# A first tile's softmax moved to ScalarE, a second tile loaded in halves, and new orders, in a fused attention and channel-mix kernel

## The chip, the cores and the metric

The kernel runs on one core of one Trainium2 chip. The metric is device time in microseconds (us) for one execution. TensorE (PE) multiplies, VectorE (DVE) and ScalarE (ACT) do the elementwise work, SyncE (SP) issues the DMA transfers, GpSimd (POOL) does almost nothing here. PEld in a row is PE's weight load.

## What is computed

Chunked local attention (batch 4, 8 heads, 768 tokens, head size 64; each chunk of 32 queries sees 16 keys to the left, its own 32, 8 to the right and 8 memory keys, 64 in all), whose output is the input of a channel mix with a squared-ReLU feed-forward and a sigmoid gate. Cut to what matters:

```python
scores = scale * np.matmul(q_c, k_full.transpose(0, 1, 3, 2))
scores = scores - np.max(scores, axis=-1, keepdims=True)
a = np.exp(scores)
a = a / (np.sum(a, axis=-1, keepdims=True) + 1e-09)
out[:, :, c_start:c_end] = np.matmul(a, v_full)
...
x_prev = np.concatenate([np.zeros((B, 1, D), dtype=np.float32), x[:, :-1, :]], axis=1)
xk = mu_k * x + (1.0 - mu_k) * x_prev
xr = mu_r * x + (1.0 - mu_r) * x_prev
k = np.maximum(xk @ w_k, 0.0)
v = k * k @ w_v
r = 1.0 / (1.0 + np.exp(-(xr @ w_r)))
return (r * v).astype(np.float32)
```

## The kernel before

The 3072 tokens are cut into 12 units of 256 tokens, each of two tiles of 128 (tile t belongs to unit t // 2). For a tile the stages are: load of queries and keys (`qk`, L561); scores on PE into the PSUM tile `s` (L588, for tile 0 L670); softmax into `e`; transposes of `e` on PE into `pt` (L751); copies of `pt` into `aTz` (L397); the product with the values (`vw`, L745) into `px` (L771); a copy into `xT` (L397). From unit 3 on the transposes are done by a round trip through DRAM instead: DVE transposes blocks of 32 by 32 (`eT`, L900), SP writes `eD` (L907) and reads it back as `aTz` in four loads (L911). From unit 6 on the product with the values (L843) has its result turned the same way (DVE L850, write of `xD` L856, four loads into `xT` L861). Then come the mix of the unit (`xf`, or its parts `xh` and `xl`), and the three matrix products of the channel mix: `ph` (first layer, L1425 for unit 0, L1454 and L1479 later), `pr` (gate, L1359, L1368), and the second layer (`pv` L1568, L1581 for the first two units, and sums `accx`, `accy`, `accz`, L1270, later). The weights arrive in ten loads w0 to w9 (L445, L447), are put together from two 32-bit words by ACT (absolute value, L465) and DVE (mask L470, join L474), and are then split into two fp32r parts.

The softmax of tile 0 works by halves b of its heads (`first_part`, L645): DVE takes the maximum from PSUM (L679, L681), subtracts it (L688, L690), ACT does one exp over 128x256 (L693), DVE sums (L699); after both halves DVE adds 1e-9, takes the reciprocal (L701, L702) and multiplies (L706). Tile 1 does the same steps whole, 128x512 at a time (`part`, L601, L606, L612, L616 to L618, L622).

What sets the order: PE's order is written by hand, `LEAD` for the first two units, a string of `STAGES` for each later one (unit 0's string is the default). In these, h, g, v and p stand for matrix products of the channel mix, s and z for scores of later units, t, a, b, x for transposes and products with the values: in unit 5's string z is the scores of unit 8 and x the `px` of unit 7. SP's first 23 loads are put in the order of `LOADS` (q0a, q0b: halves of tile 0's load; q1, q2, ...: tiles; v: values; w: weights). Everything else is placed by the planner (`Plan`): it simulates the engines with a cost for each operation, works by due times, and writes the instructions of each engine in the order of its simulated starts; each engine then executes its own list in that order, so that an instruction which waits holds up all that follow it on its engine. The letters of `FORCE` add rules: n, j make norm and join of w0 wait in the plan for steps of tile 1; t puts both copies of tile 1's `pt` on ACT. While PE waits for its first `ph`, the kernel fills in matmuls on zeros (`warm`, L1639).

## Time and profile before

| | us |
|---|---|
| median of 3 runs | 377.25 |
| the runs | 374.96, 377.25, 377.32 |
| the profiled execution, its own time | 376.67 |
| its span, first to last instruction | 374.9 |
| PE busy in the span | 367.7 (98%) |
| DVE busy | 322.7 (86%) |
| ACT busy | 206.2 (55%) |
| DMA engines busy (queue of the data) | 47.8% |

The span is divided by what each engine did; a row of the timeline gives the start, the duration, the engine, the line of the kernel, the operation with output and inputs, and in brackets how long the engine had been idle before and what ended that. The profiled execution's own time is 1.77 us longer than its span. The rows that the argument rests on stand in a section further down.

### The profile page before, as it was taken

The page shows a single profiled execution, that of the slowest core. Times are in us where ns is not written, and L with a number is a line of the kernel's source. Part 1 is how long each engine was busy: PE and PEld are TensorE (multiplying, and loading weights), DVE is VectorE, ACT ScalarE, POOL GpSimd, SP SyncE. Part 2 cuts the span into 40 slices and gives each one's busy share as a digit, 9 for nine tenths or more (in the row PEclk, how much of TensorE's full clock was granted, in tenths as well). Part 3 has the DMA queues.
Part 4 walks back from the last instruction along what each step waited for, and adds up shares of the span by engine and source line. Part 5 has one row for each costly group of instructions (what it writes and reads, how often), then busy time and mean ns, then how long its engine had stood idle before and what let it go on. Part 6 is the DMA issues. An engine that isn't in the chain of part 4 may idle for free.

```text
span 374.9 us, 11497 instructions
## 1 busy us (share of the span) xinstructions
PE 367.7 (98%) x5084; PEld 339.6 (91%) x5084; DVE 322.7 (86%) x524; ACT 206.2 (55%) x307; POOL 2.4 (1%) x9
## 2 busy tenths in 40 slices
PE   7999999999999999999999999999999999999996
PEld 5886579988999999999999998999999999999996
DVE  3899999999999499989699997996998988788274
ACT  2797996954774386475068157238338244156260
POOL 2000000000000000000000000000000000000000
PEclk9999999999999999999999999999999999999999
DMA  7999981324701735556692485266343340400101
GB/s 287 403 417 409 389 309 71 113 87 140 274 39 72 262 120 179 215 165 240 246 278 93 153 288 179 64 220 230 127 154 115 112 169 2 143 30 0 58 1 58
DMA packets 24146, 64.78 MB, mean 173 GB/s; under 512 B 2720, under 2 KB 10784, under 8 KB 23712
## 3 DMA queue, kind: packets, MB, share of 16 engines
q1 hardware_dynamic: 24096, 64.04, 47.8%
q8 instruction: 40, 0.66, 0.7%
q14 instruction: 10, 0.08, 0.1%
HBM read 49.88 MB, written 14.16 MB: 171 GB/s over the span
## 4 chain that ended last, share of the span: by engine, by line
PE 82%; DMA 9%; DVE 5%; SPq 1%; issue 1%; ACT 0%; DVEq 0%
PE ph L1479 26%; PE pr L1368 14%; PE accy L1270 10%; PE accx L1270 7%; PE accz L1270 6%; PE pv L1581 4%; DMA raw<-in_w_k_dram 4%; PE s L588 4%; PE ph L1454 3%; PE px L771 3%; PE px L843 2%; PE pv L1568 2%; DMA qk<-in_qk_dram 2%; DMA aTz<-eD 1%; DMA xT<-xD 1%
## 5 line engine op out<-in xcount | busy, mean ns | idle before, releaser
L1479 PE MATMUL ph<-xh,wk 128*128 128x256 f32 x320 | 89.1, 278 | 0.0
L1479 PE MATMUL ph<-xh,wl 128*128 128x256 f32 x320 | 88.0, 275 | 0.0
L1479 PE MATMUL ph<-xl,wk 128*128 128x256 f32 x320 | 88.0, 275 | 0.0
L1498 ACT ACTIVATE kf<-ph 128x512 f32<-128x512 f32 x47 | 27.6, 596 | 88.7 <-PE ph L1479 88.4
L1479 PEld LDWEIGHTS ph<-xh,wk 128*128 128x128 f32 x320 | 61.4, 192 | 0.8
L1479 PEld LDWEIGHTS ph<-xh,wl 128*128 128x128 f32 x320 | 61.5, 192 | 0.0
L1479 PEld LDWEIGHTS ph<-xl,wk 128*128 128x128 f32 x320 | 61.4, 192 | 0.0
L1215 DVE TENSOR_TENSOR al<-kf,ah 128x512 fp32r<-128x512 f32 x50 | 33.6, 679 | 1.8 <-PE accz L1270 1.6
L1368 PE MATMUL pr<-wr,xh 128*128 128x512 f32 x88 | 34.1, 388 | 0.0
L1368 PE MATMUL pr<-wr,xl 128*128 128x512 f32 x88 | 33.4, 379 | 0.0
L1368 PE MATMUL pr<-wl,xh 128*128 128x512 f32 x88 | 33.4, 379 | 0.0
L397 ACT CAST ah<-kf 128x512 fp32r<-128x512 f32 x45 | 27.3, 620 | 9.7 <-DVE kf L1193 7.2
L1505 ACT ACTIVATE kf<-kf 128x512 f32<-128x512 f32 x45 | 28.1, 632 | 1.1
L1377 ACT ACTIVATE sg_sb<-pr 128x512 f32<-128x512 f32 x24 | 14.0, 597 | 20.5 <-PE pr L1368 20.3
L1270 PE MATMUL accx<-wv,ah 128*128 128x256 f32 x80 | 22.1, 276 | 0.0
L1270 PE MATMUL accx<-wv,al 128*128 128x256 f32 x80 | 22.0, 275 | 0.0
L1270 PE MATMUL accx<-wl,ah 128*128 128x256 f32 x80 | 22.0, 275 | 0.0
L588 PEld LDWEIGHTS s<-qk 64*32 64x32 f32 x1472 | 15.2, 105 | 4.0 <-issue 2.9
L1368 PEld LDWEIGHTS pr<-wr,xh 128*128 128x128 f32 x88 | 16.7, 189 | 2.5
L1368 PEld LDWEIGHTS pr<-wr,xl 128*128 128x128 f32 x88 | 16.6, 189 | 2.3
L1368 PEld LDWEIGHTS pr<-wl,xh 128*128 128x128 f32 x88 | 16.7, 189 | 1.9
L588 PE MATMUL s<-qk 64*32 64x64 f32 x1472 | 17.2, 225 | 1.1 <-DMA qk<-in_qk_dram 1.1
(165 smaller groups left out, 956.0 us busy)
## 6 DMA issues: line engine op xcount, KB each, us to landing
qk<-in_qk_dram SPq DMA_DIRECT2D x23, 768.0 KB, 6.1
vw<-in_vw_dram SPq DMA_DIRECT2D x24, 512.0 KB, 5.2
out_dram<-o SPq DMA_DIRECT2D x23, 256.0 KB, 2.4
eD<-eT SPq DMA_DIRECT2D x9, 512.0 KB, 2.7
aTz<-eD SPq DMA_DIRECT2D x36, 128.0 KB, 3.0
raw<-in_w_v_dram SPq DMA_DIRECT2D x4, 1024.0 KB, 10.2
raw<-in_w_k_dram SPq DMA_DIRECT2D x3, 1024.0 KB, 10.6
xD<-aTz SPq DMA_DIRECT2D x6, 512.0 KB, 2.6
```

Source lines behind the costliest of these rows:

```text
L397: e.copy(dst, src)
L588: nc.tensor.matmul(s5[CHUNK * j : CHUNK * (j + 1), h, d - c, r, :], *operands(ts[d], r, j, slice(64 * h, 64 * h + 64)), start=True, stop=True,
L771: nc.tensor.matmul(p3[64 * h : 64 * h + 64, 2 * g : 2 * g + 2, CHUNK * j : CHUNK * j + CHUNK], v[:, g, h, j, :], a[:, h, g, j, :], start=True,
L1215: nc.vector.tensor_sub(low(n), place[n](), T["ah", u, n].bitcast(F32))
L1270: nc.tensor.matmul(o, x, w, start=(n in fresh and c + i == 0), stop=(c == cs[-1] and i == 2), skip_group_check=True)
L1368: nc.tensor.matmul(pairs(p), x[:, place_of(u)[k], c * P : (c + 1) * P], woven(w), start=(k + n == 0), stop=(k == KT - 1 and n == 2),)
L1377: nc.scalar.activation(sg, p, AF.Sigmoid)
L1454: nc.tensor.matmul(pairs(T["ph", u, f][:, i * UTOK : (i + 1) * UTOK]), w[:, fc], x[:, :, k].rearrange("p t n -> p n t"), start=(i + k + n ...
L1479: nc.tensor.matmul(pairs(p[:, i * UTOK : (i + 1) * UTOK]), w[:, fc], x[:, :, place_of(u)[k]].rearrange("p t n -> p n t"), start=(k + n == ...
L1498: e.activation(part(), p, AF.Relu)
L1505: e.activation(q, q, AF.Square)
L1581: nc.tensor.matmul(pairs(p), x[:, tc_], woven(w), start=(f + n == 0), stop=(f == FT - 1 and n == 2),)
```

## The change

Softmax of tile 0. DVE still takes the maximum of each half, and multiplies it by minus the scale (128x4). ACT then reads the scores from PSUM and does the subtraction inside the exp, its bias being the scaled maximum: as that is another value for each head, one exp of 128x64 for each of the 8 heads (4 to a half), whose second output (`accum_out`) is the sum over the 64 keys. Subtractions and sums are gone from DVE. The scores of the second half now go to banks of the tag `tp` (two of them, by head parity), where they went to one tile of tag `s`.

Tile 1. Its load is cut into two halves (q1a, q1b), and scores, maximum, subtraction, exp and sum go by halves, still the old way (DVE subtracts, one exp, DVE sums).

Orders. `LOADS`: w0 before the identity, w3 before w4, q2 before q3, w7 before v2, w9 before v3. `LEAD`: the scores of unit 1 are split, with a quarter of the last `ph` step between; some further pairs change places. `STAGES`: other strings for all units but 1. `FORCE`: the second half of w0's absolute value now waits for tile 0's two copies of `pt`, and tile 1's copies are no longer kept on ACT. The planner's model of instruction fetches has other constants, v1's load another cost, and the planner's last pass keeps the order in which operations open a buffer tag. Four fp32 matmuls on zeros fewer are issued before the first `ph` (10, before 14).

```diff
-FORCE = "njt"
+FORCE = "njc"
 HALF = 2
-LOADS = "q0a q0b q1 id w0 v0 v1 w1a w1b w2 w4 w3 q3 q2 w5 w6 v2 w7 w8 v3 q4 w9 q5"
...
+FUSED, FUSED_US = (0,), 1.2
+LOADS = "q0a q0b q1a q1b w0 id v0 v1 w1a w1b w2 w3 w4 q2 q3 w5 w6 w7 v2 w8 w9 v3 q4 q5"
...
-    0: "z h0 h2 h3 h1 x g0 p1 p7 p6 p2 p5 g1 p3 p4",
...
+    0: "z h2 h0 h1 h3 x g0 p1 p7 p6 p4 p2 p5 g1 p3",
...
-    5: "h1 z h0 h2 x h3 p1 g0 p7 p6 g1 p5 p2 p4 p3",
...
+    5: "z h0 h1 h2 x h3 g0 p1 p7 p6 g1 p2 p5 p4 p3",
...
-FETCH, FETCH_LEAD, FETCH_US, FETCH_AT, FETCH_FROM, FETCH_RATE = 256, 40, 4.9, 123, 2600, (0.0046, 0.0088)
+FETCH, FETCH_LEAD, FETCH_US, FETCH_AT, FETCH_FROM, FETCH_RATE = 256, 32, 4.0, 123, 2600, (0.0046, 0.0088)
...
+                if s.tag in opened and opened[s.tag] is not o:
+                    edge(opened[s.tag], o)
+                opened[s.tag] = o
...
+            def f_sub(b):
+                if fused:
+                    nc.vector.tensor_scalar_mul(mxs(b), mxs(b), -SCALE)
+                    return
...
+                def sub(h, s):
+                    m = mxs(b)[:, h]
+                    nc.vector.tensor_sub(e4(b)[:, h], s, m.unsqueeze(len(m.shape)).to_broadcast(list(s.shape)))
...
+            def f_exp(b):
+                if not fused:
+                    nc.scalar.activation(e4(b), e4(b), AF.Exp, scale=SCALE)
+                    return
...
+                for h in range(2):
+                    for r in range(R):
+                        g = slice(R * b + r, R * b + r + 1)
+                        nc.scalar.activation(
+                            e4(b)[:, h, r], s4(b, h)[:, r], AF.Exp, bias=pt["mx"][:, h, g], scale=SCALE, accum_out=pt["sum"][:, h, g]
+                        )
+
+            def f_sum(b):
...
+                if not fused:
+                    nc.vector.reduce_sum(sm[:, :, R * b : R * (b + 1)], e4(b), axis=AX.X)
+                if b:
+                    nc.vector.tensor_scalar_add(sm, sm, 1e-9)
+                    nc.vector.reciprocal(sm, sm)
...
-            if t == 0:
-                l.append([op(("dma", 1.05), lambda b=b: f_load(0, b), new=[x] * (b == 0), use=[x] * b, due=0.1 * b) for b in range(2)])
-                loads.update(q0a=l[0][0], q0b=l[0][1])
+            if u == 0:
+                l.append([op(("dma", 1.05), lambda b=b, t=t: f_load(t, b), new=[x] * (b == 0), use=[x] * b, due=0.2 * t + 0.1 * b) for b in range(2)])
+                loads.update({f"q{t}a": l[t][0], f"q{t}b": l[t][1]})
```

Where instructions stand, first on DVE at the start of the program. A name carries its unit or tile, and ends with a buffer number: `mx0_0`, `s0_0_1`, `sum0_0` belong to tile 0, `mx0_1`, `s0_1`, `sum0_1` to tile 1, `e0` to both. Before, from the maximum of tile 0's second half to the last multiplication of tile 1:

```order
L681 TENSOR_REDUCE mx0_0_115<-s0_0_2_96 128x2x2
L690 TENSOR_TENSOR e0_136<-s0_0_2_96,mx0_0_115 128x2x128
L699 TENSOR_REDUCE sum0_0_143<-e0_136 128x2x2 x2
L701 TENSOR_SCALAR sum0_0_143<-sum0_0_143 128x8
L702 RECIPROCAL sum0_0_143<-sum0_0_143 128x8
L601 TENSOR_REDUCE mx0_1_189<-s0_1_148 128x8
L606 TENSOR_TENSOR e0_136<-s0_1_148,mx0_1_189 128x2x256
L706 TENSOR_TENSOR e0_136<-e0_136,sum0_0_143 128x2x256
L616 TENSOR_REDUCE sum0_1_204<-e0_136 128x8
L617 TENSOR_SCALAR sum0_1_204<-sum0_1_204 128x8
L618 RECIPROCAL sum0_1_204<-sum0_1_204 128x8
L622 TENSOR_TENSOR e0_136<-e0_136,sum0_1_204 128x2x256
```

And after the change, from the first maximum of tile 1 on (tile 0's maxima and their multiplication by minus the scale stand ahead of it):

```order
L688 TENSOR_REDUCE mx0_1_170<-s0_1_147 128x2x2
L699 TENSOR_TENSOR e0_140<-s0_1_147,mx0_1_170 128x2x128
L688 TENSOR_REDUCE mx0_1_170<-s0_1_147 128x2x2
L725 TENSOR_SCALAR sum0_0_139<-sum0_0_139 128x8
L726 RECIPROCAL sum0_0_139<-sum0_0_139 128x8
L699 TENSOR_TENSOR e0_140<-s0_1_147,mx0_1_170 128x2x128
L723 TENSOR_REDUCE sum0_1_200<-e0_140 128x2x2
L730 TENSOR_TENSOR e0_140<-e0_140,sum0_0_139 128x2x256
L723 TENSOR_REDUCE sum0_1_200<-e0_140 128x2x2
L725 TENSOR_SCALAR sum0_1_200<-sum0_1_200 128x8
L726 RECIPROCAL sum0_1_200<-sum0_1_200 128x8
L730 TENSOR_TENSOR e0_140<-e0_140,sum0_1_200 128x2x256
```

Tile 0's two sums and three subtractions are gone; tile 1's maximum, subtraction and sum each stand twice, over 128x256, and the multiplication of tile 0 (L706 before, the first L730 now) has moved from before tile 1's sum to between its two parts.

The second place is DVE at the end of unit 5, with the last steps of unit 8's softmax (`e8`), its transposes (`eT8`), and the evacuation of unit 5's results (`o5`). Before:

```order
L622 TENSOR_TENSOR e8_2667<-e8_2667,sum8_0_2969 128x1024
L1312 TENSOR_TENSOR o5_1_2916<-accz5_2897,o5_1_2916 128x256
L1032 TENSOR_TENSOR xl6_0_3017<-df6_2669,xh6_0_2914 128x1024
L1335 TENSOR_TENSOR o5_1_2916<-o5_1_2916,sg_sb_78 128x512
L1312 TENSOR_TENSOR o5_0_2867<-accy5_2920,o5_0_2867 128x256
L1340 TENSOR_TENSOR o5_0_2867<-accx5_2853,sg_sb_78 128x256
L1342 TENSOR_TENSOR o5_0_2867<-o5_0_2867,sg_sb_78 128x256
L900 STREAM_TRANSPOSE eT8_3204<-e8_2667 128x1024
L977 TENSOR_TENSOR df7_3208<-xT7_2998 128x16x63
```

And now:

```order
L629 TENSOR_TENSOR e8_2673<-e8_2673,sum8_0_2928 128x1024
L1252 TENSOR_TENSOR al2_5_2932<-kf5_1_2755,ah3_5_2969 128x512
L1069 TENSOR_TENSOR xl6_0_2986<-df6_2704,xh6_0_2904 128x1024
L1377 TENSOR_TENSOR o5_0_2911<-accx5_2887,sg_sb_78 128x256
L1349 TENSOR_TENSOR o5_1_2934<-accy5_2936,o5_1_2934 128x256
L937 STREAM_TRANSPOSE eT8_3014<-e8_2673 128x1024
L1349 TENSOR_TENSOR o5_1_2934<-accz5_2915,o5_1_2934 128x256
L1372 TENSOR_TENSOR o5_1_2934<-o5_1_2934,sg_sb_78 128x512
L1349 TENSOR_TENSOR o5_0_2911<-accy5_2936,o5_0_2911 128x256
L1379 TENSOR_TENSOR o5_0_2911<-o5_0_2911,sg_sb_78 128x256
```

Before, the transposes `eT8` came after the last instruction on `o5`, with six rows between them and `e8`'s multiplication; now four rows stand between, and four instructions on `o5` come behind the transposes.

The third place is SP's queue behind it. Before:

```order
L1315 DMA out_0_dram<-o5_1_2916 128x512
L1315 DMA out_0_dram<-o5_0_2867 128x512
L907 DMA eD8_3206<-eT8_3204 128x1024
L561 DMA qk20_3212<-in_qk_dram 128x1536
L911 DMA aTz_79<-eD8_3206 32x4x256 x4
L561 DMA qk21_3297<-in_qk_dram 128x1536
L745 DMA vw18_3307<-in_vw_dram 128x1024
```

And now:

```order
L898 DMA xT7_2906<-xD7_2874 32x4x256 x4
L944 DMA eD8_3030<-eT8_3014 128x1024
L1352 DMA out_0_dram<-o5_1_2934 128x512
L1352 DMA out_0_dram<-o5_0_2911 128x512
L948 DMA aTz_79<-eD8_3030 32x4x256 x4
L568 DMA qk20_3141<-in_qk_dram 128x1536
L568 DMA qk21_3176<-in_qk_dram 128x1536
```

The write `eD8` now stands ahead of the two stores of unit 5's output, and the load `qk20` (768 KB), which stood between the write and the four reads `aTz`, now stands behind them.

## Rows read from the trace of the kernel before

**Rows 1.** stretch, its length, busy PE, PEld, DVE, ACT, POOL, PEclk, DMA share, GB/s

```profile
...
0.00:16.56 16.56, 13.87 (x229) 10.62 (x229) 9.54 (x25) 6.97 (x12) 2.33 (x8) 1.00 0.90 338
16.56:224.10 207.54, 207.43 (x2987) 187.64 (x2984) 192.53 (x294) 131.96 (x195) 0.11 (x1) 1.00 0.58 209
224.10:226.10 2.00, 0.82 (x34) 0.50 (x37) 0.73 (x3) 1.69 (x4) 0.00 (x0) 1.00 0.46 177
226.10:371.70 145.60, 145.60 (x1870) 140.87 (x1850) 119.47 (x205) 65.59 (x99) 0.00 (x0) 1.00 0.31 105
```

**Rows 2.** PE's waits, longest first (line, releaser: us in total, times, longest)

```profile
...
PE px L843 <- DMA aTz<-eD: 1.2, 2, 0.6
PE s L588 <- DMA qk<-in_qk_dram: 1.1, 1, 1.1
```

**Rows 3.** timeline of the start (start us, us, engine, line, operation, idle before)

```profile
...
1.18 2.93 PE L1639 MATMUL warm<-zero_sb 128*128 128x256 f32 x6 [1.18 <-DVE zero_sb L387]
...
4.98 0.68 PE L670 MATMUL s<-qk 64*32 64x48 f32 x32 [0.25 <-DMA qk<-in_qk_dram]
...
5.59 1.97 PE L1639 MATMUL warm<-zero_sb 128*128 128x256 f32 x6
...
7.77 0.20 DVE L702 RECIPROCAL sum<-sum 128x8 f32<-128x8 f32 x1
```

**Rows 4.** the timeline going on, 8 to 17 us

```profile
...
8.64 0.85 PE L588 MATMUL s<-qk 64*32 64x64 f32 x64 [1.08 <-DMA qk<-in_qk_dram]
...
9.42 2.43 PE L1639 MATMUL warm<-zero_sb 128*128 128x256 f32 x10
...
12.81 0.69 DVE L622 TENSOR_TENSOR e<-e,sum 128x512 f32<-128x512 f32 x1
...
13.55 0.66 PE L751 MATMUL pt<-id_sb,e 128*128 128x128 f32 x4
...
14.25 1.17 ACT L397 COPY aTz<-pt 64x512 f32<-64x512 f32 x2
14.26 1.23 DVE L474 SCALAR_TENSOR_TENSOR w<-w,raw 128x1024 uint32<-128x1024 uint32 x1
...
15.47 1.15 PE L771 MATMUL px<-aTz,vw 128*64 128x64 f32 x32 [0.18 <-ACT aTz L397]
...
16.56 0.71 PE L1425 MATMUL ph<-xf,w 128*128 128x128 f32 x4
```

**Rows 5.** durations by shape, 0 to 20 us (line, operation, count, busy us, mean ns)

```profile
...
L693 ACT ACTIVATE e<-e 128x256 f32<-128x256 f32 x2 | 0.8, 417 | 4.2 <-DVE e L688 3.7 <-DVE e L690 0.5
...
L950 ACT ACTIVATE xf<-px,mu_sb 128x128 f32<-128x128 f32 x2 | 0.7, 368 | 0.0
...
L681 DVE TENSOR_REDUCE mx<-s 128x4 f32<-128x256 f32 x1 | 0.4, 425 | 0.1
```

**Rows 6.** timeline, 28 to 30 us: PE and its weight loads

```profile
...
28.52 1.32 PEld L588 LDWEIGHTS s<-qk 64*32 64x32 f32 x128 [0.33 <-DMA qk<-in_qk_dram]
28.52 1.48 PE L588 MATMUL s<-qk 64*32 64x64 f32 x128
...
29.93 1.13 PE L1425 MATMUL ph<-xf,w 128*128 128x256 f32 x4
```

**Rows 7.** DVE's timeline before the wait at 225 us

```profile
...
213.63 0.42 DVE L1342 TENSOR_TENSOR o<-o,sg_sb 128x256 f32<-128x256 f32 x1
213.96 1.24 DVE L900 STREAM_TRANSPOSE eT<-e 128x1024 f32<-128x1024 f32 x1
```

**Rows 8.** SP's DMA issues, same stretch (start us, us of issuing)

```profile
...
215.60 0.45 SPq L561 DMA_DIRECT2D qk<-in_qk_dram  x1
218.12 2.88 SPq L911 DMA_DIRECT2D aTz<-eD  x4
```

**Rows 9.** chain that ended last, 200 to 230 us (start us, us, what)

```profile
...
220.56 5.28 DMA aTz<-eD
```

**Rows 10.** DMA issues, from the page's last part (count, KB each, median us to landing)

```profile
...
aTz<-eD SPq DMA_DIRECT2D x36, 128.0 KB, 3.0
```

More of the change, by code (lines that the diff above doesn't have):

```diff
@@ L151, in place @@
             if eng == "pe":
-                cost, _ = self.fetched(t, cost, port)
+                o.ready = max([0.0] + [e + HOP[g] for e, g in ready if g != "pe"])
+                cost, _ = self.fetched(t, cost, port, o.ready)
             elif port:
```

154 lines of the change are left out of this document (80 added, 74 removed), and 10 rows, old and new, of the table STAGES.

## The prediction

> **What bounds the kernel now.** I read first the busy times by stretch, then PE's waits, then the timeline of the two places where PE waits. Between 16.56 us, where the first `ph` matmul starts, and 224.1 us PE is busy 207.43 of 207.54 us; from 226.1 us to its end at 371.7 us it is busy 145.60 of 145.60 us; only around 225 us does it stand, 1.18 of 2.00 us [rows 1]. The list of waits says the same: the longest is that of `px` for `aTz`, 1.2 us in two pieces, and the next, 1.1 us for `qk`, lies in the start [rows 2, 4]. So the time is the start of the first `ph` (16.56), the PE work behind it, the 1.2 us, and the 3.2 us from PE's last matmul to the span's end at 374.9. An edit to another engine gains only what it takes from the start or from that one wait, and loses what it adds as a new wait of PE. DVE is busy 192.53 of the 207.54 us [rows 1], so there is little room for it to be late.
>
> The start is a chain through tile 1. PE waits for tile 1's load until 8.64 and scores for 0.85 us; the last of the softmax ends at 12.81 + 0.69 = 13.50; `pt` follows at 13.55; ACT copies it in 14.25 to 15.42; `px` runs from 15.47 and the first `ph` from 16.56. Beside it the join of w0, which `ph` also needs, ends at 15.49 [rows 4]. Tile 0 isn't on this chain: its sums and reciprocal are done by 7.97 [rows 3], before tile 1's scores begin.
>
> The wait at 225 us is a chain too: DVE finishes unit 5's output at 214.05, transposes `e8` from 213.96 [rows 7], SP writes it to DRAM, issues another 768 KB load at 215.60, and issues the four reads at 218.12 to 221.00 [rows 8]; the last read takes 5.28 us from 220.56 and lands at 225.84 [rows 9].
>
> **The change, part by part.** The sums are made against the profiled execution, 376.67 us, which lies 0.58 under the median.
>
> *Tile 0 on ACT.* DVE loses three subtractions and two sums, and gains two multiplications over 128x4, no dearer than the reciprocal of 0.20 [rows 3]. All that lay before 8.64, when DVE waits for tile 1 in any case, so it gives nothing by itself. ACT's price is open, since no exp with a bias and a second output stands in the trace. From below, the eight do the work of two 128x256 exps, 0.83 us; from above, each costs as much as a whole one, 8 x 0.417 = 3.3 us [rows 5]. I take 0.30 each, a little under the 128x128 one of 0.368, so 2.4 us. The second half's scores end at 4.98 + 0.68 = 5.66 [rows 3]; the first exp starts near 5.5, so they end at 7.9, or at 8.8 from above. The reciprocal that reads the sums stands behind tile 1's second maximum, near 9.6 (below), so the work is hidden at either bound; only if tile 1 landed over 1 us earlier would it show. The Trainium skill, in "ScalarE: Activation LUTs", What ACT_TABLE_LOAD costs, speaks against such a split: an ACTIVATE whose bias is a pointer has some 280 ns of fixed cost beside 0.833 ns per element, by which the eight take 8 x 0.333 = 2.7 us where two took 0.83. The trace shows no such form; by that rule the end is 8.2, and the sum the same.
>
> *Tile 1 in halves.* The first half's maximum and subtraction are done while the second half lands. If that lands when the whole did, its scores start at 8.64 and take half of 0.85, to 9.1. Then DVE has, up to tile 1's last multiplication: maximum 0.42, add 0.2, reciprocal 0.2, subtraction 0.42, sum 0.42, multiplication of tile 0 0.69, sum 0.42, add 0.2, reciprocal 0.2, multiplication 0.69. With 0.42 for each half [rows 5], 0.69 for each whole [rows 4] and the reciprocal's 0.20, for the adds too [rows 3], that is 3.9 us, less some 0.3 as neighbours overlap: it ends at 12.7, before 13.50. The gain is 0.8, and 0.5 if nothing overlaps. The second half's exp runs beside tile 0's multiplication.
>
> *The copies.* One of tile 1's two copies goes to DVE, so they run side by side instead of 1.17 us in a row on ACT [rows 4]. But the second half of w0's absolute value has to stand behind tile 0's copies on ACT, and holds tile 1's copy there until about 13.9; the join, 1.23 us, starts then and ends at 15.1, ready before it is needed. `px` of tile 1 starts near 14.7 and takes 1.15. The first `ph` comes at 15.9, a gain of 0.7; bounds 0.4 and 0.9.
>
> *What is left of it.* At 28.52 the scores of unit 1 wait for the later of the two loads q2 and q3 [rows 6]. DMA is full in the start (share 0.90 over 16.56 us [rows 1]) and the bytes ahead of the later load are the same after the change, so it lands at the same moment: the 0.7 us are lost there again. What the change gives at this place is its split: before, both tiles' scores stood behind the landing, 28.52 to 29.93, when `ph` went on; after, one tile's alone, which as a block of its own took 0.85 for tile 1 [rows 4], so `ph` goes on at 28.52 + 0.85 + 0.1 = 29.5. The lead is 0.4. Each half is a block of its own now, which costs 2 x 0.85 - 1.48 = 0.22 of PE time [rows 4, 6]; it is in the 0.4. If the load were a little earlier the lead would grow to the 0.7 of the start less 0.2; if `ph` of the fourth weight waits for its join, it shrinks to nothing.
>
> *The wait at 225 us.* `eT8` no longer stands behind the last four instructions on `o5`, of which the last ends at 214.05 [rows 7]; I put it 2 to 3 us earlier. Its write then doesn't wait behind the output's stores, and the 768 KB load that was issued between write and reads comes behind the reads. The reads are issued when the stores are, near 214 to 216, and even with 5.28 us from issue [rows 9] the last lands by 221.5, some 3 us before 224.1, where `px` was due. The 1.2 us are gone; at the least 0, if `eT8` moves by less than 1.2.
>
> *Other orders.* The remaining strings change places of equal blocks on a PE that has no wait there; they cost nothing as long as DVE, ACT and the loads keep ahead, and what they cost otherwise is a rival.
>
> Sum: 376.67 - 0.4 - 1.2 = 375.1. Against the median, 377.25, the same 1.6 us would give 375.6; I put 375.2.
>
> **The rivals.**
>
> *The load comes early (chance 0.15).* The same program ran in 374.96 and in 377.3, and what varies is most likely the start, since nothing else waits on DMA but 1.2 us. In such a run tile 1 lands earlier, and the halves shorten a chain that is then DVE's own. From 374.96 the 1.2 us still go, and a lead of 0 to 0.4: 373.4 to 373.8. Against it: two runs of three were slow ones, and the median goes with them.
>
> *PE runs at its slow pace in the start (0.17).* This one ends slower than before. The warm matmuls between tile 0's and tile 1's scores, 5.59 to 7.56, are gone, and so PE has nothing from 5.66 until tile 1's halves. The granted clock reads 1.00 in the whole stretch [rows 1], the level of 2.4 GHz, but the same matmul takes 2.93 / 6 = 0.49 us at 1.18, 0.33 at 5.59 and 0.24 at 9.42 [rows 3, 4]: it gains its pace by being busy. If it is still at 0.49 when the five warm ones in front of tile 0's transposes start at 9.1, these take 4.9 us, to 14.0, where 2.43 were enough; two transposes (0.66 each), a warm one (0.98), half of the copies (0.7) and `px` (1.15) put the first `ph` at 18.3, 1.8 later than before. Behind it PE would wait for no load up to 29.9, which gives back 0.3 of it, and the split costs 0.2: 376.67 + 1.7 - 1.2 = 377.2, and up to 378 with the first `ph` at that pace. It decides from the point where the first `ph` comes 1.2 us later than before. "TensorE: Matmul & The Clock Gate" of the Trainium skill, What's actually happening, has it that PE's clock is halved by default and released by activity; the warm rows agree.
>
> *The wait at 225 us stays (0.10).* The last read took 5.28 us where the median of all is 3.0 [rows 9, 10], so the DMA engines were crowded; if the stores now delay them as much, the time is 376.67 - 0.4 = 376.3.
>
> *A new wait (0.13).* DVE gets two copies of `pt` of about 0.6 us each between 12 and 40 us, where before it did none, and every block of PE in its new place wants its inputs earlier or later than before. A wait as long as the copies, 1.2, gives 376.3; two, 377.5.
>
> **How the numbers follow.** The forecast, a short lead and no wait at 225 us, has the remaining 0.45; its own range is 374.4 to 375.9 by the bounds above (no lead to 0.5 of it, and the 0.58 between profiled run and median). The range reaches down to 373.2, for the early load, and up to 377.6, for most of the slow pace and of the new waits; some 0.15 is left out. Within 1% of 377.25, about what a measurement of this kernel can tell from no change, means 373.5 to 381.0: faster takes half of the early load and a bit of the forecast's tail, 0.12; slower wants several new waits, 0.03; the same has 0.85.
>
> **What would show it.** In the profile after: tile 1's last multiplication ending near 12.7; the first `ph` near 15.9; `ph` behind the second scores of unit 1 near 29.5; no wait of `px` for `aTz` in PE's list; and PE busy without a gap from there on. The eight exps should end before 9.6. The warm matmuls in front of the first transposes at 0.24 say that the pace is kept; 0.4 or more says the slow rival. I am wrong if PE's list of waits has a new line of over 0.5 us behind 30 us, or if the first `ph` is later than 16.56.

## The result and the profile after

The changed kernel takes 377.85 us (median of 9 runs, 376.58 to 379.83); the kernel before, run between them, 376.05 (9 runs, 374.92 to 377.32). The ratio over the runs is 1.0066, with an interval of 1.0044 to 1.0087 (the two medians alone give 1.0048): it is slower, by less than 1%. The forecast was 375.2, in a range of 373.2 to 377.6; the time lies above the range.

The profiled execution took 378.18 us. Two lines of its page:

```profile
span 376.3 us, 11501 instructions
...
PE 367.4 (98%) x5076; PEld 339.0 (90%) x5076; DVE 321.9 (86%) x526; ACT 209.1 (56%) x322; POOL 2.7 (1%) x9
```

PE's waits after the change, longest first (line, releaser: us in total, times, longest):

```profile
PE s L673 <- DMA qk<-in_qk_dram: 2.1, 3, 1.3
PE s L595 <- issue: 1.4, 1, 1.4
...
PE px L808 <- issue: 0.6, 2, 0.4
PE accy L1307 <- DVE o L1349: 0.2, 1, 0.2
```

The wait of `px` for `aTz` [rows 2] is gone. In its place stand a stop of 1.4 us, called "issue" (PE waits for nothing that the profile shows), and 0.2 us for DVE. The rest is in the start. Its timeline after (start us, us, engine, line, operation, idle before):

```profile
5.50 1.28 ACT L714 ACT_TABLE_LOAD   x1 [5.50 <-DVE mx L692]
5.84 0.46 PE L673 MATMUL s<-qk 64*32 64x64 f32 x32 [0.44 <-DMA qk<-in_qk_dram]
6.80 0.32 ACT L714 ACTIVATE e<-s,mx 128x64 f32<-128x64 f32 x1
7.01 0.19 ACT L714 ACTIVATION_READ_ACCUMULATOR e<-s,mx 128x1 f32 x1
...
7.64 0.58 PE L673 MATMUL s<-qk 64*32 64x64 f32 x32 [1.33 <-DMA qk<-in_qk_dram]
...
8.15 3.94 PE L1676 MATMUL warm<-zero_sb 128*128 128x256 f32 x10
...
8.27 0.43 DVE L699 TENSOR_TENSOR e<-s,mx 128x256 f32<-128x256 f32 x1 [1.42 <-PE s L673]
...
9.03 0.24 ACT L714 ACTIVATION_READ_ACCUMULATOR e<-s,mx 128x1 f32 x1
...
9.31 0.17 DVE L725 TENSOR_SCALAR sum<-sum 128x8 f32<-128x8 f32 x1 [0.28 <-ACT e L714]
...
10.25 0.68 DVE L730 TENSOR_TENSOR e<-e,sum 128x512 f32<-128x512 f32 x1
...
11.74 0.69 DVE L730 TENSOR_TENSOR e<-e,sum 128x512 f32<-128x512 f32 x1
11.93 0.60 PE L788 MATMUL pt<-id_sb,e 128*128 128x128 f32 x4
...
12.56 1.18 ACT L404 COPY aTz<-pt 64x512 f32<-64x512 f32 x2 [1.55 <-PE pt L788]
...
13.76 0.69 ACT L472 ACTIVATE w<-raw 128x512 f32<-128x512 f32 x1
...
14.48 0.58 ACT L404 COPY aTz<-pt 64x512 f32<-64x512 f32 x1
...
17.08 1.16 PE L1462 MATMUL ph<-xf,w 128*128 128x128 f32 x8
...
27.75 0.86 PE L595 MATMUL s<-qk 64*32 64x64 f32 x64
...
30.39 1.13 PE L1462 MATMUL ph<-xf,w 128*128 128x256 f32 x4
```

Three things to see. The five warm matmuls (x10: each leaves two records) take 3.94 us; ten records took 2.43 before [rows 4]. Tile 0's `e` is finished at 10.25 + 0.68 = 10.93, but its transposes `pt` can't start until the warm ones ahead of them are through, at 11.93; the copies, the absolute value and the next copy follow one another on ACT. And DVE's subtraction of tile 1's first half waits 1.42 us for PE's scores of the second half. The first `ph` starts at 17.08, where before it was 16.56 [rows 4].

The same stretch by windows (length, busy PE, PEld, DVE, ACT, POOL, granted clock, DMA share, GB/s):

```profile
6.00:8.00 2.00, 0.67 (x64) 0.51 (x52) 0.59 (x2) 1.99 (x10) 0.00 (x0) 0.96 1.05 396
8.00:10.00 2.00, 2.00 (x20) 1.51 (x5) 1.41 (x6) 1.58 (x10) 0.00 (x0) 0.50 0.95 363
10.00:12.00 2.00, 2.00 (x8) 1.61 (x7) 1.90 (x7) 0.97 (x2) 0.53 (x2) 0.69 1.03 424
```

The granted clock is 0.50 from 8 to 10 us: the level of 1.2 GHz, and 0.69 in the mean of the next window. In 6 to 8 us, just ahead, PE was busy for only 0.67 of 2.00 us. Before, the clock read 1.00 over the whole start [rows 1].

**Where the time went, in the two profiles.** PE's last matmul starts at 372.72, before at 371.43: 1.29 later. `ph` goes on behind the second scores of unit 1 at 30.39, before at 29.93 [rows 6]: 0.46 of it is the start. Behind that I compare the starts of PE's matmuls of the same number, counted from the last one. At 60 us the changed kernel is 0.50 late (a `pv` matmul at 50.75 comes 0.62 behind the one before it, where its neighbours are 0.22 apart, but only 0.04 of that is left there). The stop at 185 us brings it to 2.09, the wait of `accy` at 213 to 2.54; the wait at 225 us that is gone brings it back to 1.04, and two small pieces near 258 and 343 us (0.15 and 0.09) make up the rest. By this count a stop costs more than the idle time that its row shows: 1.59 for the 1.38 at 185 us, 1.50 for the 1.18 at 225 [rows 1].

**A fairer "before".** The profiled execution of before was one with a late load: tile 1's scores started at 8.64 [rows 4]. In three later profiles (e5 and e12 with the old start, e2 with three warm matmuls fewer) the first `ph` came at 15.1 to 15.2; in e5, below, tile 1's scores started at 7.17 and `ph` went on at 29.12. The changed kernel also had its load early (second half's scores at 7.64). Beside an undisturbed old start, the new one loses 2.0 us at the first `ph` and 1.27 at 30 us.

### The profile page after: what moved, and what is told of

The parts are those of the page before. It is cut to its first block, busy times and chain, and to the rows that moved or that the text cites. A ratio compares the mean times of both kernels' runs of the same rounds, so it can differ in the third digit from the quotient of the medians.

```text
span 376.3 us, 11501 instructions
## 1 busy us (share of the span) xinstructions
PE 367.4 (98%) x5076; PEld 339.0 (90%) x5076; DVE 321.9 (86%) x526; ACT 209.1 (56%) x322; POOL 2.7 (1%) x9
## 4 chain that ended last, share of the span: by engine, by line
PE 82%; DVE 9%; DMA 4%; SPq 2%; issue 1%; ACT 1%; DVEq 0%
PE ph L1516 26%; PE pr L1405 13%; PE accy L1307 9%; PE accz L1307 6%; PE accx L1307 6%; PE pv L1618 4%; PE s L595 3%; PE px L808 3%; PE ph L1462 3%; PE ph L1491 3%; PE pv L1605 2%; DMA xD<-aTz 2%; PE px L880 2%; DVE al L1252 2%; DMA qk<-in_qk_dram 1%
## 5 line engine op out<-in xcount | busy, mean ns | idle before, releaser
L404 ACT CAST ah<-kf 128x512 fp32r<-128x512 f32 x43 | 26.4, 621 | 17.0 <-DVE kf L1230 8.5
```

The lines of the kernel that those rows point to most:

```text
L404: e.copy(dst, src)
```

## The experiments

Medians stand beside those of the kernel before on the same chip. The theories: (1) PE's slow pace in the start; (2) ACT's new work, or the halves, make the start late; (3) the new strings cost PE waits; (4) the lead of the new `LEAD` is worth what was predicted.

### The wait at 225 us alone: e5

```diff
 # before
-    5: "h1 z h0 h2 x h3 p1 g0 p7 p6 g1 p5 p2 p4 p3",
+    5: "z h0 h1 h2 x h3 g0 p1 p7 p6 g1 p2 p5 p4 p3",
```

> The kernel before with unit 5's string of the change and nothing else; the start is that of before. In it the transposes eT8 and the write eD8 stand ahead of the output's stores, and the 768 KB load behind the reads, as in the changed kernel. If the wait of px8 at 225 us was worth what the prediction said, it goes and the time falls by 1.2 to 1.35 from before (375.7 to about 374.4). Rival: the wait goes but PE finds another one of about 1 us nearby, and the time stays within 0.4 of before.

374.88 us (10 runs, 374.41 to 375.93) beside 375.56 (14 runs): 0.9982 [0.9965, 1.0000]. PE's waits in its profile:

```profile
PE warm L1639 <- DVE zero_sb L387: 1.2, 1, 1.2
PE ph L1425 <- DVE w L474: 0.5, 1, 0.5
PE s L670 <- DMA qk<-in_qk_dram: 0.3, 1, 0.3
PE px L771 <- ACT aTz L397: 0.2, 1, 0.2
```

All four lie in the start; behind it PE never stands. The wait is gone and nothing has taken its place: 0.7 us in the medians. That it is not 1.2 fits two other profiles with the old string of unit 5: in e2 and e10 `px` waits 0.52 and 0.68 us there, so the 1.18 of the profiled execution was a long wait. Of all versions run this is, with e15, the best, below both kernels; 1.0000, the end of its interval, only just reaches no change.

### PE's pace in the start: e7, e9, e1, e4, e2, e10

**e7**: three warm matmuls instead of five ahead of tile 0's `pt`; the one ahead of tile 1's `pt` stays.

```diff
 # changed kernel
+                nth += 1
+                if nth in (5, 6):
+                    n = 3 if nth == 5 else 1
```

> The changed kernel with three warm matmuls instead of five in front of tile 0's transposes. Theory: these stand in PE's order ahead of the transposes, and at the slow pace (0.43 for a half, 0.86 for one) five take 3.9 to 4.6 us and hold the transposes up beyond the end of tile 0's multiplication at 10.9; three take at most 2.6 and don't. The first transposes then start at 11.0 (11.93 to 12.5 before), the first ph at 15.8 to 16.4 (17.08 to 17.5), and the time falls by 0.7 to 1.2, to about 376.9. Rival: without them PE is slow for longer, the products with the values and the first ph run at the slow pace, and the time doesn't fall by more than 0.3.

The start did what was expected: first `ph` at 16.13, `ph` going on at 29.82, with `pt` waiting for DVE and no longer for PE. The time did not: 379.63 (4 runs), 1.0107 [1.0064, 1.0149]. The profile shows why (timeline of PE near 257 us):

```profile
257.50 0.33 PE L880 MATMUL px<-vw,aTz 64*32 64x64 f32 x12 [2.55 <-issue]
```

A stop like the one at 185 us, larger and at another place.

**e9**: e7 with ten tiny warm matmuls (32x32) between the halves of tile 1's scores, 40 instructions more.

```diff
 # e7
-                if nth in (5, 6):
-                    n = 3 if nth == 5 else 1
+                n = {4: 10, 5: 3}.get(nth, n)
...
+                    p, w = (32, 32) if nth == 4 else (P, 2 * P)
```

> The changed kernel with three warm matmuls in front of tile 0's transposes, as in e7, and ten tiny ones (32x32, 40 PE instructions of some 0.02 us each) between the halves of tile 1's scores, where PE waits 0.6 us for DVE's maximum anyway. PE then has 18 warm matmuls' worth of instructions ahead of the first ph, as in e4, in which PE stopped at neither 185 nor 256 us; in e7 it stopped 2.5 us at 255. Theory (late fetches of PE's instructions, whose borders move with the number of instructions ahead of them): the start is that of e7 (first ph 15.9 to 16.5), the stops marked issue at 185 and 255 are gone or under 0.3 us, and the time falls by 2 to 3.5 from e7's 379.63, to 376 to 377.5. Rival (the number of instructions is nothing to it): a stop of over 1 us in the scores or the px near 185 or 255, and 379 to 380 as e7.

377.33 (10 runs), 1.0039 [1.0013, 1.0065]. First `ph` at 16.01, `ph` going on at 29.70, no "issue" stop left; one new wait of PE:

```profile
PE pt L788 <- DVE e L730: 1.2, 2, 0.9
...
PE pr L1405 <- ACT kf L1535: 1.0, 1, 1.0
```

Beside e7 the start is the same and the stop of 2.5 us is gone. So the stop depends on the number of PE's instructions ahead of it, or on the times that go with it; the strings' section comes back to this, and to the wait for `kf`.

**e1**: three full warm matmuls between tile 1's halves, where the diff took three away.

```diff
 # changed kernel
+                nth += 1
+                if nth == 4:
+                    n = 3
```

> The changed kernel with three warm matmuls (12 PE instructions) put back, between the two halves of tile 1's scores. Theory 1, PE's clock: in the changed kernel the granted clock fell to 0.50 at 8 to 10 us and 0.69 at 10 to 12, and the five warm matmuls took 3.94 us where 2.43 were enough; here the clock stays at 1.00 there, the warm ones take about 2.2 us, the first ph comes near 16.0 instead of 17.08, and the time falls by 0.6 to 1.0 to about 377.0. The stop of PE at 185 us stays, 1.5 us. Theory 2, the start is late because ACT's table load waited until 5.50 and its exps end at 9.27: the clock rises, but the first ph stays near 17.0 and the time is the changed kernel's, 377.85.

378.98 (6 runs), 1.0081 [1.0054, 1.0108]: a miss. The three took 2.93 us, 0.49 a record, and held the second half's scores to 9.59; the five behind them then ran in 2.42, but the first `ph` came at 17.51. Bringing back the pace in this way cost as much as it gave.

**e4**: eight narrow ones (128x64) at the same place.

```diff
 # changed kernel
+                if nth == 4:
+                    n = 8
...
+                    w = 64 if nth == 4 else 2 * P
```

> The changed kernel with eight narrow warm matmuls (128x64, 32 PE instructions) between the two halves of tile 1's scores: where e1 moves all later PE instructions by 12 places, this moves them by 32. Theory 1 for the stop at 185 us (a late fetch of a block of instructions): the block's border moves to about 0.3 us earlier in the scores of unit 7 and its fetch is asked for about 2 us earlier, so the stop shrinks by more than half or goes, with the same DMA jam. Rival (the stop is a wait for data or for the DMA jam itself): it stays at 1.4 to 1.7 us. For the start: the granted clock stays at 1.00 until 12 us if narrow matmuls keep PE's pace as wide ones do, and falls if they don't.

380.02 (6 runs; 379.86 without the longest, 383.68), 1.0096 [1.0065, 1.0127]. They took 3.67 us, the second half's scores waited until 11.03, the first `ph` came at 19.61. The stop at 185 was gone, as in e9, but PE stood 2.29 us in front of a `pr` at 203.10.

**e2** takes from the kernel before the three warm matmuls that stood between the scores of tile 0 and tile 1; **e10** leaves their number and makes them tiny (32x32), so the instruction count is that of before.

```diff
 # before; e2:
+                if nth == 3:
+                    n = 0
 # e10:
+                n = {3: 3}.get(nth, n)
...
+                    p, w = (32, 32) if nth == 3 else (P, 2 * P)
```

> The kernel before without its three warm matmuls between the scores of tile 0 and tile 1; nothing else. Theory 1 (PE's clock): the granted clock falls below 1.00 somewhere between 8 and 14 us, the warm matmuls before the first transposes take 3.5 us or more instead of 2.43, the first ph comes 0.5 to 1.5 us later than 16.56, and the time rises by 0.3 to 1.0 over the kernel before. Theory 2 (ACT): no change in the time; the warm matmuls were filling only.

> The kernel before with its three warm matmuls between tile 0's and tile 1's scores made tiny (32x32): PE has nothing to do there, as in e2, but all later instructions stand at the place of before, where in e2 they stood 12 earlier. It splits e2's loss of 1.2 us. If the loss is that of PE's pace, runs with a mean clock of 0.995 or less come up here too, and the median is 376.3 to 377. If it is that of late fetches, the median is before's 375.6 within 0.4, and the stops of 0.2 to 0.3 us at 254 and 271 us that e2 shows are gone.

e2: 376.91 (12 runs) beside 375.71, 1.0032 [1.0010, 1.0054]. e10: 376.75 (10 runs) beside 375.60, 1.0022 [0.9996, 1.0049]. Both lose about 1.2 us in the medians, though e10's interval reaches no change. e2's profiled execution kept its pace (warm 2.43, first `ph` 15.22), but in 5 of its 12 runs the mean granted clock of the run was at most 0.995, and in 4 of 10 of e10; in none of 23 runs of before, whose lowest was 0.998. These runs are not slower than the others, though (medians of 377.25 against 376.91 in e2, 376.37 against 376.86 in e10), so the mean clock doesn't sort out the loss. e10's profile is one of these (0.995); its timeline of PE, then its windows:

```profile
8.07 3.78 PE L1642 MATMUL warm<-zero_sb 128*128 128x256 f32 x10
```

```profile
6.00:8.00 2.00, 0.91 (x64) 0.84 (x64) 1.63 (x6) 0.44 (x2) 0.26 (x2) 0.86 1.06 408
8.00:10.00 2.00, 2.00 (x15) 1.57 (x6) 1.78 (x3) 0.37 (x1) 0.00 (x0) 0.50 0.97 399
```

The clock is at 0.50 at the same place as in the changed kernel, and the first `ph` comes at 16.53, though tile 1's scores began at 7.09, earlier than e5's. So at an unchanged count of instructions the lost pace makes the start late: by 1.43 us beside e5 at the first `ph`, and by 0.70 where `ph` goes on (29.82). That it is also what costs the runs their 1.2 us is argued and not shown: e2's profile lost nothing at the start (`ph` going on at 29.11). "TensorE: Matmul & The Clock Gate" of the Trainium skill, What's actually happening, calls the low clock the default, which activity releases; these rows agree.

### The strings: e3, e8, e6, e12

**e3**: unit 4's old string in the changed kernel.

```diff
 # changed kernel
-    4: "h0 a b h1 h2 h3 p1 z p7 g0 p2 p6 x p5 g1 p4 p3",
+    4: "h0 a b h1 h2 h3 p1 z p7 g0 p6 x g1 p2 p5 p4 p3",
```

> The changed kernel with unit 4's string of before (px of unit 6 after p6, ahead of p2's and p5's products, as before), all else new. Theory 1: PE's stop of 1.59 us at 185 us is a fetch of instructions that came late, behind a jam of DMA traffic (the write xD6 took 6.0 us, the load of v17 6.8, the write eD7 6.2, where 2.6 to 2.9 are usual), and the jam is made by unit 4's new order; here these take their usual time, PE doesn't stop at 185, px8 still doesn't wait at 225, and the time falls by 1.2 to 1.8, to about 376.3. Rival: the stop is bound to the place of the scores and the number of instructions ahead of them, and stays 1.0 us or more; the time stays within 0.5 of 377.85.

377.01 (12 runs) beside 375.71, 1.0035 [1.0015, 1.0055]: 0.84 less than the changed kernel's median, but 0.5 less when each is taken against the before beside it, and the intervals overlap. PE at 184 to 188 us, the changed kernel first, then e3:

```profile
184.06 1.35 PE L595 MATMUL s<-qk 64*32 64x64 f32 x113
186.78 0.34 PE L595 MATMUL s<-qk 64*32 64x64 f32 x15 [1.38 <-issue]
187.06 0.38 PE L1516 MATMUL ph<-xh,wk 128*128 128x256 f32 x1
```

```profile
184.70 1.49 PE L595 MATMUL s<-qk 64*32 64x64 f32 x128
186.12 0.38 PE L1516 MATMUL ph<-xh,wk 128*128 128x256 f32 x1
```

The block is cut after 113 of its 128 matmuls, at a place where nothing that the kernel wrote makes it wait. The DMA queues in 180.0 to 184.4 us and (changed kernel alone) 184.4 to 187.0, q8 being the one that brings instructions (packets, MB, share of 16 engines):

```profile
q1 hardware_dynamic: 385, 1.42, 90.7%
...
q1 hardware_dynamic: 119, 0.18, 20.8%
q8 instruction: 1, 0.02, 2.3%
```

```profile
q1 hardware_dynamic: 246, 0.88, 50.8%
q8 instruction: 1, 0.02, 1.2%
```

With the new string a load, a write of `xD` and a write of `eD` fall together: `xD` took 6.0 us and `eD` 6.2, where before both took 2.6. In the changed kernel no instruction packet came while the data took 90.7%, and PE went on 2.4 us after 184.4; in e3 it came in time. I infer that PE had run out of instructions; no row says so outright.

The traces say more for it than this one place. q8 brings 40 packets of 16 KB in every run. In the changed kernel, e1 and e8, which differ by up to 20 instructions ahead of it, PE stops at 185 us behind the same count of its matmuls and weight loads, 5266 or 5267, in the middle of a block, and goes on 1.33 to 1.43 us after the end of q8's 20th packet. In e6, e7 and e8 it stops at 257 us behind 7551 to 7553, and goes on 1.40 to 1.53 after the end of the 29th. The waits in front of `pr` in e4, e9 and e16 (2.29, 1.04 and 0.78 us) all come behind 5776, 1.48 to 1.64 after the end of the 22nd; the profile puts them down to ACT, but to `ah` in e4 and to `kf` in the others. The string alone doesn't make the stop: in e12, below, the same string in the kernel before has `eD` at 5.0 us and the data queue at 76.1% from 179.8 to 184.2, but the 20th packet ended at 182.81, and PE didn't stop.

"Runtime: NRT & Kernel Launch" of the Trainium skill, Instruction fetch mechanics, has the crossing from one block of instructions to the next mostly hidden; if these stops are such crossings, it cost 1.38 us here, and 2.55 in e7.

The profile of e3 had the start at the slow pace all along: ten warm records in 4.63 us, first `ph` at 17.51. Its four windows from 6 to 14 us read a granted clock of 1.00 nevertheless: there the slow pace could be read from the length of the warm rows alone.

**e8**: e7's warm matmuls and e3's string together.

```diff
 # changed kernel
+                if nth in (5, 6):
+                    n = 3 if nth == 5 else 1
...
+    4: "h0 a b h1 h2 h3 p1 z p7 g0 p6 x g1 p2 p5 p4 p3",
```

> Both repairs on the changed kernel: three warm matmuls in front of the first transposes, and unit 4's string of before. If the start and PE's stop at 185 us are what made the change slower, the two gains add up: 377.85 - 0.8 (measured for the string) - 0.7 to 1.2 = 375.9 to 376.3, about the kernel before's 375.7. If they don't add, 377.0, as with the string alone.

378.61 (6 runs), 1.0067 [1.0044, 1.0090]. The two don't add: PE stands at 186 (0.64), 213 (0.51) and 258 us (1.82), and behind the last the granted clock was 0.50 from 260 to 262 us.

**e6**: all old strings in the changed kernel. **e12**: all new strings in the kernel before.

```diff
 # e6: the changed kernel; e12 the reverse, in before
-    0: "z h2 h0 h1 h3 x g0 p1 p7 p6 p4 p2 p5 g1 p3",
+    0: "z h0 h2 h3 h1 x g0 p1 p7 p6 p2 p5 g1 p3 p4",
...
```

> The changed kernel with all strings of before for the later units; its start (softmax on ACT, halves, loads, lead) is the changed one. Expected: PE's stop at 185 us (1.6) and the wait for accy at 213 (0.4) go, the wait of px8 at 225 (1.35) comes back; about 377.2 against 377.85. The first ph stays late, 16.9 to 17.6, and all of what is left over before (1.5 us) is the start. Rival: if the start is not what costs, the time comes down to before's 375.7 to 376.0.

> The kernel before (its start, its softmax, its loads) with all of the change's strings for the later units. It shows the strings without the start. Theory: px8 doesn't wait at 225 (-0.7 as in e5), but unit 4's string makes the jam at 179 to 188 us, and PE stops at 185 for 0.5 to 1.6, and waits 0.3 to 0.5 for accy at 213; time 375.6 to 376.6, no better than before. Rival: the strings are a gain as a whole and only the start is bad: 374.3 to 375.0, as e5.

e6: 379.38 (4 runs), 1.0096 [1.0071, 1.0121]. e12: 377.18 (10 runs) beside 375.60, 1.0034 [1.0007, 1.0060], with a start like e5's (first `ph` 15.10, going on at 29.26). So the strings other than unit 5's cost the old kernel about 2.3 us beside e5. In e12 the expected stop at 185 us did not come. In the changed kernel the old strings are no better, where 377.2 was expected: e6 stands at 121 us (0.89, for DVE's `o`) and 257 (0.57), and its profiled execution had the slow start of e3 (first `ph` 17.33). e12's largest wait behind the start:

```profile
211.86 0.35 PE L1270 MATMUL accy<-wv,ah 128*128 128x256 f32 x1 [0.81 <-DVE o L1312]
```

`accy` needs the buffer that DVE's addition into `o5` empties. In e5 it is not waited for there; the changed kernel has the same wait at 213.08, of 0.21.

### ACT, the halves and the lead: e13, e14, e16, e11, e15

**e13**: e5 with tile 0's softmax on ACT, tile 1 whole and the old orders. **e14**: e13 with an exp of one column at the very start.

```diff
 # e13: e5
+FUSED, FUSED_US = (0,), 1.2
...
+                        nc.scalar.activation(
+                            e4(b)[:, h, r], s4(b, h)[:, r], AF.Exp, bias=pt["mx"][:, h, g], scale=SCALE, accum_out=pt["sum"][:, h, g]
+                        )
 # e14: e13
+    nc.scalar.activation(tbl, zero_sb[:, :1], AF.Exp)
```

> The kernel of e5 (before, with unit 5's new string) with tile 0's softmax on ACT, and that alone: tile 1 whole, loads, lead, warm matmuls (14) and strings as in e5. Theory (ACT's sums come late): the table load waits behind DVE's first maximum and runs at about 5.6 to 6.9, the exps end near 9.3 where DVE's sums of before were done at 7.5 to 8.0; DVE's add and reciprocal, which stand ahead of tile 1's maximum, hold that up from 8.1 to 9.7; the first transposes come 1 to 1.6 us later than in e5 (10.22), and the time rises by 0.4 to 1.5 from e5's 374.88. Rival (the work on ACT is hidden, as the prediction had it): the first transposes at 10.2 to 10.5 and the time within 0.3 of e5.

> e13 with one more exp of a single column on ACT at the very start, so that ACT's table is loaded before the first scores are there. If it is the late table load that makes the sums late, the exps start at 5.6 and end near 8.0, DVE's maximum of tile 1 starts within 0.4 of e5's 8.07, and the time is within 0.4 of e5's. If it is the eight exps themselves (0.29 each, 2.4 us in all), it stays 0.3 to 0.8 us behind e5 at the first transposes.

e13: 379.38 (8 runs) beside 375.85, 1.0091 [1.0065, 1.0116]. Its timeline:

```profile
5.57 1.28 ACT L712 ACT_TABLE_LOAD   x1 [5.57 <-DVE mx L690]
...
6.86 0.32 ACT L712 ACTIVATE e<-s,mx 128x64 f32<-128x64 f32 x1
7.17 0.30 ACT L712 ACTIVATE e<-s,mx 128x64 f32<-128x64 f32 x1
...
9.37 0.17 DVE L723 TENSOR_SCALAR sum<-sum 128x8 f32<-128x8 f32 x1 [2.92 <-ACT e L712]
9.70 0.64 DVE L602 TENSOR_REDUCE mx<-s 128x8 f32<-128x512 f32 x1
```

With DVE's old order the sums are wanted before tile 1's maximum, and DVE stands 2.92 us for them; the maximum comes at 9.70, in e5 at 8.07. `ph` goes on at 30.11, 1.0 later than e5's 29.12. PE also stops for 1.96 us at 195.42 ("issue"), which e5 doesn't. This stop is not like the one at 185 us. PE's queue holds a wait for semaphores of 3.95 us there, which ends with DVE's subtraction of unit 7's softmax; the new plan has put that subtraction behind other work of DVE, at 194.10, where e5 has it at 185.76:

```profile
194.10 1.22 DVE L607 TENSOR_TENSOR e<-s,mx 128x1024 f32<-128x1024 f32 x1
...
195.42 0.80 PE L878 MATMUL px<-vw,aTz 64*32 64x64 f32 x48 [1.96 <-issue]
```

So e13 doesn't price the softmax on ACT alone: 0.98 us of its loss beside e5 stands at `ph`, and 2.1 come from this reordering.

e14: 378.50 (10 runs), 1.0062 [1.0036, 1.0087]. The table is loaded at 0.73, the eight exps are done by 8.17, 1.17 earlier, and still its first `ph` came at 16.89: in this execution the warm matmuls at 5.64 ran at 0.49 a record (2.93 us for six) and held tile 1's scores to 8.50. The stop at 195 us stays (1.96, again up to the end of DVE's subtraction, 195.38).

**e16**: e9 with the same early exp.

```diff
 # e9
+    nc.scalar.activation(tbl, zero_sb[:, :1], AF.Exp)
```

> e9 (the changed kernel, three warm matmuls in front of the first transposes, ten tiny ones between the halves) with the early table load of e14. In e9 DVE had two waits in a row: its subtraction on tile 1's first half waited 1.40 us, until 8.55, for PE's scores of the second half, which stand in the same PSUM tile, and its add until 9.40 for ACT's last exp (0.1). If the table were what holds the start up, the first transposes would move from 11.28 to 10.3 or earlier. Theory: the halves' common tile holds it up, and they move by no more than 0.3; the time within 0.4 of e9's 377.33.

376.91 (10 runs: nine of 374.76 to 380.38, one of 382.76), 1.0020 [0.9983, 1.0057], no clear difference from before. The exps end at 8.08, 1.2 earlier than in the changed kernel, and DVE's subtraction of tile 1's first half still waits 1.40 us for PE, as long as in e9; the first transposes start at 11.43 (e9 11.28), the first `ph` at 16.20. So where tile 1 goes by halves, the scores are what DVE waits for, and ACT costs it little (0.28 us in the changed kernel).

**e11**: e9 with tile 0's softmax the old way, meant to show the halves alone.

```diff
 # e9
-FUSED, FUSED_US = (0,), 1.2
+FUSED, FUSED_US = (), 1.2
```

> As e9, but tile 0's softmax is done the old way (DVE subtracts and sums, two exps on ACT), by halves: the rest of the change as it is, the same warm matmuls. It prices the softmax on ACT. From the changed kernel's trace: the exps, held up by ACT's table load that now waits behind the first maximum (5.50 to 6.78), end at 9.27, and DVE's reciprocal waited 0.28 us for them; on the other side DVE has 1.2 us less to do between 5 and 10 us. Theory: the softmax on ACT is worth 0.3 to 0.8 us at the first transposes, but not in the end, since the later of the loads q2 and q3 is waited for: within 0.5 of e9. Rival: DVE's list is what the start waits for, and e11 is slower than e9 by 0.8 or more.

381.10 (4 runs), 1.0142 [1.0095, 1.0189]. It shows nothing of the halves: the planner put DVE's copy of tile 0's `pt` ahead of tile 1's multiplication, `pt` of tile 1 came at 16.10, and the first `ph` at 21.41.

**e15**: e5 with the change's `LOADS` and `LEAD`, tile 1's load whole.

```diff
 # e5
-LEAD = "... h0.2.0 h0.3.0 s1.0 s1.1 h0.3.1 ...
+LEAD = "... h0.2.0 s1.0 h0.3.0 s1.1 h0.3.1 ...
```

> The kernel of e5 with the change's LOADS and LEAD (tile 1's load whole), and nothing else: the softmax of before, its FORCE, 14 warm matmuls. From the traces: the changed lead lets ph go on behind the second scores of unit 1 at 29.0 to 29.4 if the first ph comes at 15.1 (in e5 29.12), and the pv at 50 us waits 0.3 us for DVE in every kernel with the new lead (50.13 to 50.75 in the changed one). Theory: no gain from it, 374.9 to 375.5. Rival: it is worth the 0.4 us that the prediction gave it: 374.4 to 374.6, and ph behind the scores at 28.7.

375.02 (10 runs), 0.9977 [0.9953, 1.0002]. The first `ph` came 0.28 later than in e5 and `ph` went on 0.10 earlier, at 29.02: 0.38 won between. But that is not the split: e5's `ph` waited 0.48 us in this stretch for a join of weights (its second wait in the list above), e15's did not, and the split itself cost 0.10. In neither did the scores of unit 1 wait for a load. The small gain holds until 212 us (`pv` comes 0.40 late at 49.37, as in the changed kernel, and nearly all of that is made up by 60 us), and is lost in two pieces near 216 and 254 us (0.12 and 0.42), the second at an "issue" stop of 0.20 in `px`; PE's last matmul starts 0.46 later than in e5. Beside e5 no gain is left.

## Why the prediction failed, step by step

The sum had two gains, 0.4 for the lead and 1.2 for the wait, and put the other orders at nothing. In the two profiles the lead came out as a loss of 0.46 and the wait as a gain of 1.50; the other orders cost 2.3: 1.59 at the stop of 185 us, 0.45 at `accy`, 0.28 in small pieces. So two terms failed: the lead, through the start in front of it, and the orders, which cost the most.

**The wait at 225 us: right.** `eT8` and its DMAs in the changed kernel, on DVE and on SP:

```profile
212.85 1.24 DVE L937 STREAM_TRANSPOSE eT<-e 128x1024 f32<-128x1024 f32 x1
```

```profile
214.11 0.34 SPq L944 DMA_DIRECT2D eD<-eT  x1
215.15 1.13 SPq L1352 DMA_DIRECT2D out_dram<-o  x2
217.18 1.75 SPq L948 DMA_DIRECT2D aTz<-eD  x4
```

The transposes came 1.1 us earlier than before [rows 7] while PE ran later; counted from the start of `px` that was due (224.1 before, 226.91 now) they moved by 3.9, where I had 2 to 3. The reads were issued from 217.18, all behind one another, and landed by 222.0; `px` started at 226.91 without a wait. Of the 1.2 us, e5 shows 0.7 in the medians, as the wait was long in the profiled execution.

**Tile 1 in halves: failed.** I had the first half's maximum and subtraction done while the second half lands. From the start of the last scores to the end of the last multiplication, before took 13.50 - 8.64 = 4.86 us [rows 4] and the changed kernel 12.43 - 7.64 = 4.79; I had 12.7 - 8.64 = 4.06. The maximum was done in time (6.43 to 6.85), but the subtraction waited 1.42 us for the scores of the second half, which PE writes into the same PSUM tile. The diff shows that tile: I counted DVE's work and not the tile that it shares. So the subtraction (0.34 until the next step) fell behind the scores, DVE waited 0.28 for ACT's sums, and the half's scores took 0.58 where I had 0.46: with these the 0.73 is named. In e6, e7 and e8 the tile holds PE up too: the second half's scores wait 0.59 to 0.63 us for DVE's maximum of the first. No run gave the halves tiles of their own, so that the tile is the cause is read from these waits. The halves gave 0.07 of the 0.8, and the end at 12.43, close to the 12.7 named, was luck: it came from an earlier load.

**The copies: failed through PE.** From the last multiplication to the first `ph` it was 3.06 us before [rows 4] (and 3.06 in e5), and 4.65 after; I had 3.2. Tile 0's `pt` came 1.0 us after its input was ready, behind the warm matmuls, and everything on ACT slid with it. The rival of the slow pace said this with its mechanism, in the rows it named; its price, 377.2 to 378, holds the median of 377.85, but by luck: the first `ph` came at 17.08 and not at 18.3 (its own terms add up to 18.15), and what made up the difference were the orders, which it left out. The sign named for it, 0.4 or more for a warm record, read 0.39. Its chance of 0.17 looks too small: that PE would have nothing to do between the scores was certain from the diff, and the rows showed 0.49, 0.33 and 0.24 in order of how long it had been busy; but e2's profile shows that the pace can be kept even so. Its decision point, a first `ph` 1.2 later than before, was not reached against the profiled one (0.5) but was against e5 (2.0).

**Tile 0 on ACT: size right, place wrong.** The exps come 0.29 apart (6.80, 7.10, and so on to 8.84), and take 2.47 us in all; I had 0.30 and 2.4. But the table load, 1.28 us, which before ran at 0.73 while ACT had nothing to do, now stands behind the first exp's own wait for DVE, and the sums are there at 9.27 instead of 7.9. With the halves' order DVE lost 0.28 to that; with the old order 2.92 (e13). "Hidden at either bound" came near to holding only because the subtraction was late too. "ScalarE: Activation LUTs" of the Trainium skill, What ACT_TABLE_LOAD costs, gives some 1283 ns for the load, as the row does; the step lacked its place, not its size.

**The lead: failed.** The 0.38 of e15, where I had 0.4, is a likeness by luck: it came from a wait for a join that went away. The split could give nothing where no load is waited for. In the changed kernel `ph` goes on at 30.39 and not at 29.5: PE arrived at unit 1's scores at 27.75 and waited for no load there. The step that "the 0.7 us are lost there again" took the load as the bound; with a late start PE itself was.

**The other orders: wrong.** "They cost nothing" was worth 2.3 us in e12 against e5. The rival of a new wait (0.13) had the size, 1.2 for one, but not the kind: beside waits for DVE's additions into `o`, the largest were stops without a named cause, 1.38 of idle time in the changed kernel, at a fixed count of PE's instructions and behind a packet of instructions. A term put at nothing on a PE without a wait left out that these, too, have to come in time.

Beside e5, then, the changed kernel's last matmul starts 372.72 - 369.21 = 3.51 later: 1.27 from the start and 2.24 behind it, of which 1.58 at the stop of 185 us and 0.45 at `accy`.

**What stays open.** That PE ran out of instructions at 185 and 257 us was inferred, from counts and packets, and not seen; nor does a run tell why a packet came late in one execution and not in another. e9's wait of 1.0 us at 198 us has the same signs, but it stands at the start of a block, where ACT, which the profile names, can't be ruled out. The halves by themselves were not measured (e11's plan put DVE's steps in another order), and the softmax on ACT only together with a reordering of DVE. Why e2 and e10 lose 1.2 us in the medians is shown for the start of one execution alone. No run put the changed kernel's losses right all together: e9 and e16, the best of its repairs, stay above e5.

## What to carry to other kernels

Work that only keeps TensorE busy is work in its queue: where a change takes some away, read from the rows at which pace the rest will run, and what stands behind it. When a step is split so that a first half can run early, check each tile that both halves share, and each one-time cost (a table load) that will now stand behind a new first instruction. On an engine that is busy 98% of the time a new order has no free moves: change one string, time it, and keep it only if nothing new waits; here one string of seven gave the only gain seen. And where a stop has no named cause, compare it over several runs by the count of PE's instructions ahead of it, and look in the queue for a wait for semaphores: that told the stop at 185 us from the one at 195.

## What the runs showed of the hardware

An exp with a second output is two instructions: the ACTIVATE of 128x64 (0.31 to 0.35 us) and an ACTIVATION_READ_ACCUMULATOR (0.19 to 0.24); they overlap, and the pair comes every 0.29 us. The table load moved with the first exp: at 0.73 us before, at 5.50 after, behind the wait for DVE's maximum, and at 0.73 again with a one-column exp at the start (e14). And PE's loss of pace doesn't show as idle time: from 8 to 10 us it is busy for 2.00 of 2.00 us at the low clock. The length of its rows tells, and the granted clock not always (0.50 in the changed kernel, 1.00 in e3 with records as long). A packet of PE's instructions that ended late was followed by PE going on 1.33 to 1.53 us after its end (six stops in five profiles).
